# W_out's preparation, additions to the total, decodings, dense sums and last token pieces at other places of the phases

## The chip, the cores and the metric

The kernel runs on one core of one Trainium2 chip. The metric is the device time of one execution in microseconds (us), as the median of several runs of the same program. The engines are called PE (matrix multiplication), DVE (the vector engine), ACT (the scalar engine), POOL (GpSimd) and SP (the engine whose queue issues the kernel's DMAs). Each engine works through its own list of instructions in order.

## The reference, cut to what matters

Three layers follow each other: a linear attention with a decaying state, a mixture of 8 experts in which every expert sees every token, and a dense layer with a leaky activation.

```python
def reference(...):
    x = _attn_ref(q, k, v)              # (2, 8, 768, 64) -> 1536 tokens x 512
    x = _moe_ref(x, w_gate, w1, w2)
    return _moe2_ref(x, w_in, w_out, alpha)

def _moe_ref(x, w_gate, w1, w2):        # N 1536, D 512, E 8, F 1024
    P = np.exp(logits - logits.max())   # then 8 rounds of row and column scaling
    for e in range(E):
        h = np.maximum(x @ w1[e], 0.0)
        out += P[:, e:e + 1] * (h @ w2[e])

def _moe2_ref(x, w_in, w_out, alpha):   # d_ff 2048
    h = x @ w_in
    g = np.maximum(h, 0.0) + alpha * np.minimum(h, 0.0)
    return (g @ w_out).astype(np.float32)
```

## The kernel before

After the attention, the work is cut into 20 phases. Phases 0 to 7 are the experts for the 768 tokens of batch 0 and phases 8 to 15 the experts for those of batch 1. Phases 16 and 17 are the two halves of the dense layer for batch 0, phases 18 and 19 those for batch 1. `E` is 8, so `ph == E + 3` is phase 11. Phases from 8 on are called fast: there both matrix products are done with seven block products where eight would be needed, and every number is split in a high and a low part, so that one product is three matmuls (high by high, high by low, low by high).

A fast phase has 56 positions, and each holds six matmuls of 128x128 by 128x384 columns. Positions 0 to 26 and 29 are the products of the first layer, called (j, p) with j from 0 to 3 and p from 1 to 7; positions 27, 28 and 30 to 55 are those of the second layer, numbered u from 0 to 27 (`fast2`). Product (j, 6) makes a partial result E out of bank B by a DVE addition (line 931), and (j, 7) goes on adding into bank B, so PE has to wait until DVE has read it. In the same way DVE evacuates (j, 7) from B (line 940) before (j, 4) adds to it.

All other work hangs on positions. `step(ph, pos, fn)` says that `fn` is recorded behind the matmuls of that position. This sets only the order in which each engine's instructions stand in its queue; when one runs follows from its queue and from what it waits for. A fast phase's other work is:

- `decode_at`: one unit of W_in or W_out, which comes as 64-bit numbers, is turned into float32. Its four positions are for three DVE passes (lines 832, 834, 837), one ACT pass (842), two DVE passes (850, 853), and a store that also starts the load of the next unit (858, 822). The buffer `rd` that the next unit lands in is a single one. There are 32 units, 18 of them in phases 8 to 15.
- `dense_prep(i)`, i from 0 to 7 for phases 8 to 15: a quarter of a half of W_out is loaded (248), split on ACT and DVE (253, 257) and stored (275, 276), then four sums are made on POOL (267), split again, and stored (273). Its six positions are for the load, the high part with a store, the low part with a store, the four sums, the second high part and the second low part.
- `gather(m, h)`: an expert's weighted result `t` is added to `total` on POOL (1075), eight such additions a phase, in the phase after the one that made them.
- `t1` to `t4` (990, 995 or 997, 1009) make the second layer's combined inputs from the hidden blocks b11, b12, b21 and b22 on DVE; `hhigh(k)` (1017, ACT) and `hlow(k)` (1025, DVE) split input k, of 14, into the tile `hs`, which has five buffers. Input k is used by u = 2k and u = 2k + 1. In the dense phases the activation costs another ACT pass (902) and DVE pass (903) for each block.
- `x_keep(3, ...)`: the tokens of batch 1 for the dense layer, the last token pieces. Fourteen pieces are made in phases 16 and 17 from `total`: a POOL subtraction (349), a high part on ACT (353), a low part on POOL (357), a store (360). The tile `xs` of these pieces has two buffers. `x_fetch` (365) loads the finished pieces at the end of phase 17. `x_keep(2, ...)` does the same for batch 0 in phases 9 to 14.
- `w1_at`: the next phase's first-layer weights. In phases 15 to 19 they need four POOL sums each (`w1_sum`, 129).

```python
        def step(ph, pos, *fns):
            if pos >= 60:
                ph, pos = ph + 1, pos - 60
            for fn in fns:
                at(ph, seq[ph][pos], fn)
```

Of the kernel before, what the change touches and what calls it, by code (L numbers as in the profile page):

```python
# [23 lines left out]
E, F = 8, 1024  # L24
# [22 lines left out]
def tile_kernel(ctx, tc, lead, qkT, kv, ctab, w_gate, w1, w2, w_in, w_out, alpha, out):  # L47
# [349 lines left out]
    with tc.manual_schedule():  # L397
# [774 lines left out]
# [5 lines that stand above are left out]
# [27 lines left out]
        for ph in range(len(PHASES)):  # L1204
# [28 lines left out]
            if fast:  # L1233
                w1_at(ph, n + 2, pool, dve, 0, 3, 4, 4, 6, 9, 10)
                w1_at(ph, n + 3, pool, dve, 5, 10, 12, 11, 13, 16, 17)
                w1_at(ph, n + 4, pool, dve, 24, 36, 38, 39, 40, 42, 43)
                w1_at(ph, n + 5, pool, dve, 34, 44, 45, 48, 49, 50, 52)
            else:
# [27 lines left out]
            if fast:  # L1266
                if ph in (E + 3, E + 6):
                    decode_at(ph, 4, 5, 6, 8)
                    decode_at(ph, 13, 14, 15, 17)
                    decode_at(ph, 24, 25, 26, 28)  # L1270
                else:
                    decode_at(ph, 5, 7, 8, 10)
                    decode_at(ph, 19, 21, 23, 25)
                if E + 1 < ph < 2 * E:
                    for q in range(8):
                        step(ph, (2, 5, 8, 11, 14, 17, 20, 24)[q], lambda m=q // 2, h=q % 2: gather(m, h))
                if ph < 2 * E:
                    step(ph, 0, lambda ph=ph: weight_load(ph))
                    if ph == E:
                        keys = ((ph, 6), (ph, 13), (ph, 24), (ph, 27), (ph, 36), (ph, 40))  # L1280
                    elif ph == E + 1:
                        keys = ((ph - 1, 50), (ph, 3), (ph, 14), (ph, 15), (ph, 24), (ph, 27))
                    else:
                        keys = ((ph - 1, 38), (ph - 1, 46), (ph, 2), (ph, 3), (ph, 20), (ph, 23))
                    for (q, pos), fn in zip(keys, dense_prep(ph - E)):
                        step(q, pos, fn)
                dense = ph >= 2 * E
                p2, p3, q3 = (24, 33, 35) if dense else (21, 25, 31)
                for pos, fn, jp in ((17, t1, 0), (p2, t2, 0), (p3, t3, 0), (27, t1, 1), (30, t2, 1), (q3, t3, 1)):
                    step(ph, pos, lambda ph=ph, fn=fn, jp=jp: fn(ph, jp))  # L1290
                h2, h4 = (21, 29) if dense else (19, 22)
                l2, l4 = (23, 30) if dense else (20, 24)
                highs = (11, 25, h2, 28, h4, 31, 32, 34, 36, 38, 41, 43, 47, 49)
                lows = (13, 26, l2, 29, l4, 32, 33, 35, 37, 39, 42, 44, 48, 50)
                for k in range(14):
# [6 lines left out]
                if ph == 2 * E:  # L1302
                    for k in range(2):
                        step(ph, 3 + k, lambda k=k: x3.append(x_keep(3, k, *x_copy(k, total))))
                    for i, key in enumerate((29, 33, 38, 42, 46, 50, 66, 73, 80, 86, 90, 94, 97, 100)):
                        for q, pos in enumerate((0, 2, 3, 5)):
                            to = key + pos
                            step(ph + to // 56, to % 56, lambda i=i, q=q: x3[i % 2][i // 2][q]())
# [8 lines left out]
            if ph + 1 in XGROUP:  # L1317
                g = XGROUP[ph + 1]
                if g > 1:
                    for i, pos in enumerate((20, 21, 22, 23, 25, 26, 28, 30, 38, 40, 45, 46, 50, 51)):  # L1320
                        q = (B11, T1, T2, B21, T3, T4, B22)[i // 2]
# [143 lines left out]
```

## Time and profile before

| | before |
|---|---|
| time, median of 3 runs | 1299.54 us (1299.24 to 1300.45) |
| the profiled execution, its time | 1297.32 us |
| the profiled execution, its span | 1295.6 us |
| PE busy | 1263.1 us (97%) |
| DVE busy | 1035.4 us (80%) |
| ACT busy | 632.6 us (49%) |
| POOL busy | 450.8 us (35%) |
| moved by DMA | 379.21 MB |

The span runs from the first to the last instruction of the profiled execution; its own time is 1.7 us longer, and it lies 2.2 us under the median of the runs. A busy share is an average over stages with different limits. Because PE does the same matmuls in each fast phase, a phase that is longer than the shortest one shows by how much PE was made to wait or ran slower.

### The profile page before, as it was taken

The page shows a single profiled execution, that of the slowest core. Times are in us where ns is not written, and L with a number is a line of the kernel's source. Part 1 is how long each engine was busy: PE and PEld are TensorE (multiplying, and loading weights), DVE is VectorE, ACT ScalarE, POOL GpSimd, SP SyncE. Part 2 cuts the span into 40 slices and gives each one's busy share as a digit, 9 for nine tenths or more (in the row PEclk, how much of TensorE's full clock was granted, in tenths as well). Part 3 has the DMA queues.
Part 4 walks back from the last instruction along what each step waited for, and adds up shares of the span by engine and source line. Part 5 has one row for each costly group of instructions (what it writes and reads, how often), then busy time and mean ns, then how long its engine had stood idle before and what let it go on. Part 6 is the DMA issues. An engine that isn't in the chain of part 4 may idle for free.

```text
span 1295.6 us, 20588 instructions
## 1 busy us (share of the span) xinstructions
PE 1263.1 (97%) x7358; PEld 1192.6 (92%) x7358; DVE 1035.4 (80%) x1546; ACT 632.6 (49%) x1153; POOL 450.8 (35%) x414
## 2 busy tenths in 40 slices
PE   9999999999999999999999999999899998989998
PEld 7889898989898989899999999999899998979998
DVE  6677888988888888657779787879787978686867
ACT  5634543435352625354546453546354455645653
POOL 5734161707071625001123413242404435554110
PEclk9999999999999999999999999999999999998999
DMA  9785999999999999799897989899798956687625
GB/s 357 263 262 158 329 340 336 340 332 348 337 342 341 337 332 338 251 367 345 280 393 250 377 279 337 279 322 305 272 329 280 341 196 211 230 278 256 181 81 179
DMA packets 231158, 379.21 MB, mean 293 GB/s; under 512 B 16992, under 2 KB 135824, under 8 KB 231056
## 3 DMA queue, kind: packets, MB, share of 16 engines
q1 hardware_dynamic: 231056, 377.90, 85.7%
q8 instruction: 58, 0.95, 0.3%
q14 instruction: 44, 0.36, 0.1%
HBM read 243.59 MB, written 132.67 MB: 290 GB/s over the span
## 4 chain that ended last, share of the span: by engine, by line
PE 73%; DVE 12%; DMA 7%; issue 4%; ACT 2%; SPq 1%; POOL 1%; DVEq 0%; ACTq 0%; POOLq 0%
PE B L288 8%; PE B L289 8%; PE B L290 8%; PE o L288 5%; PE o L290 5%; PE o L289 5%; PE A L289 5%; PE A L288 5%; PE A L290 5%; PE D L290 3%; PE E L288 3%; PE E L289 3%; PE E L290 3%; PE D L288 3%; PE D L289 3%
## 5 line engine op out<-in xcount | busy, mean ns | idle before, releaser
L1017 ACT ACTIVATE hs<-b 128x768 fp32r<-128x768 f32 x168 | 140.2, 842 | 92.4 <-DVE b L990 43.3
L1025 DVE TENSOR_TENSOR hs<-b,hs 128x768 fp32r<-128x768 f32 x144 | 154.4, 1077 | 19.8 <-ACT hs L1017 18.7
L129 POOL TENSOR_TENSOR raw<-raw 128x256 f32<-128x256 f32 x136 | 133.6, 992 | 104.9 <-DMA raw<-wd 46.9
L288 PE MATMUL B<-xh,W 128*128 128x384 f32 x440 | 150.0, 341 | 7.5 <-DVE E L931 4.0
L290 PE MATMUL B<-xh,W 128*128 128x384 f32 x440 | 147.8, 336 | 0.0
L289 PE MATMUL B<-xl,W 128*128 128x384 f32 x440 | 147.7, 336 | 0.0
L224 POOL TENSOR_TENSOR pr<-pr 128x256 f32<-128x256 f32 x52 | 51.9, 999 | 190.4 <-DMA pr<-in_w_dram 62.9
L149 ACT ACTIVATE W<-raw 128x512 fp32r<-128x512 f32 (+1 forms) x144 | 98.5, 694 | 19.4 <-DVE raw L129 19.3
L288 PE MATMUL A<-xh,W 128*128 128x384 f32 x320 | 107.6, 336 | 0.0
L290 PE MATMUL A<-xh,W 128*128 128x384 f32 x320 | 107.4, 335 | 0.0
L289 PE MATMUL A<-xl,W 128*128 128x384 f32 x320 | 107.1, 335 | 0.0
L288 PE MATMUL B<-hs,ws 128*128 128x384 f32 x288 | 97.9, 340 | 8.9 <-ACT hs L1017 7.3
L289 PE MATMUL B<-hs,ws 128*128 128x384 f32 x288 | 97.8, 340 | 1.8 <-DVE hs L1025 1.8
L928 ACT ACTIVATE B<-A 128x384 f32<-128x384 f32 x80 | 38.3, 478 | 123.9 <-PE A L290 120.4
L1075 POOL TENSOR_TENSOR total<-total,t 128x384 f32<-128x384 f32 x54 | 73.8, 1390 | 67.3 <-DVE t L1055 64.2
L290 PE MATMUL B<-hs,ws 128*128 128x384 f32 x288 | 97.1, 337 | 0.0
L931 DVE TENSOR_TENSOR E<-B,d 128x384 f32<-128x384 f32 x80 | 45.1, 563 | 64.8 <-PE B L290 58.7
L267 POOL TENSOR_TENSOR dr<-dr 128x256 f32<-128x256 f32 x32 | 29.3, 917 | 190.7 <-DVE dw L257 147.7
L288 PEld LDWEIGHTS B<-xh,W 128*128 128x128 f32 x440 | 82.7, 188 | 12.8 <-DVE E L931 6.8
L159 POOL TENSOR_TENSOR W<-raw,W 128x512 fp32r<-128x512 f32 (+1 forms) x49 | 76.3, 1572 | 38.2 <-ACT W L149 19.2
L159 DVE TENSOR_TENSOR W<-raw,W 128x512 fp32r<-128x512 f32 (+1 forms) x95 | 86.8, 929 | 2.8 <-ACT W L149 2.8
L289 PEld LDWEIGHTS B<-xl,W 128*128 128x128 f32 x440 | 82.8, 188 | 0.3
(492 smaller groups left out, 3690.4 us busy)
## 6 DMA issues: line engine op xcount, KB each, us to landing
ws<-c SPq DMA_DIRECT2D x168, 512.0 KB, 6.5
raw<-in_w_dram SPq DMA_DIRECT2D x64, 512.0 KB, 5.8
c<-W SPq DMA_DIRECT2D x64, 384.0 KB, 6.5
W<-c SPq DMA_DIRECT2D x88, 256.0 KB, 6.4
pr<-in_w_dram SPq DMA_DIRECT2D x32, 512.0 KB, 6.1
c<-pw SPq DMA_DIRECT2D x32, 512.0 KB, 7.2
c<-pr SPq DMA_DIRECT2D x32, 512.0 KB, 7.9
raws<-in_w_dram SPq DMA_DIRECT2D x32, 384.0 KB, 5.7
```

Source lines behind the costliest of these rows:

```text
L129: eng.tensor_tensor(out=out, in0=in0, in1=in1, op=op)
L149: nc.scalar.activation(out=hi, in_=src, func=AF.Copy)
L159: eng.tensor_tensor(out=lo, in0=src, in1=hi.bitcast(F32), op=ALU.subtract)
L224: eng.tensor_tensor(out=out, in0=in0, in1=in1, op=op)
L288: nc.tensor.matmul(ps, ah, bh, start=first, stop=False, skip_group_check=True)
L289: nc.tensor.matmul(ps, ah, bl, start=False, stop=False, skip_group_check=True)
L290: nc.tensor.matmul(ps, alo, bh, start=False, stop=last, skip_group_check=True)
L928: nc.scalar.activation(out=banks[n, "B"], in_=banks[n, "A"], func=AF.Copy)
L931: nc.vector.tensor_tensor(out=banks[n, "E"], in0=banks[n, "B"], in1=banks[n, "d"], op=add)
L1017: nc.scalar.activation(out=t[:, 0, :], in_=hsource(ph, k), func=func)
L1025: nc.vector.tensor_tensor(out=lo, in0=src, in1=hi.bitcast(F32), op=ALU.subtract)
L1075: eng.tensor_tensor(out=dst, in0=dst, in1=tt[m, h], op=ALU.add)
```

## The change

All edits are numbers of positions, and rules by phase that choose them. No operation is added or taken away.

- The POOL sums of the next phase's first-layer weights stand at 18 and 28 and no longer at 24 and 34.
- Three units are decoded in phases 8 and 9, no longer in 11 and 14. In 8 and 9 they begin at positions 5, 17 and 29.
- The eight additions to the total stand in pairs at 2, 5, 8 and 11, no longer one by one up to 24.
- W_out's preparation has the same six positions in all its phases, 6, 12, 24, 27, 40 and 52. From phase 10 on its load and first split stood in the phase before, and its sums at 3.
- In the dense phases `t2` and `t3` and the parts of inputs 2 and 4 stand where they stand in the expert phases.
- The last token pieces begin at 8 of phase 16, no longer at 29, with wider spaces, and end at 42 of phase 17 and no longer at 49. The last pieces of a group of tokens are fetched at up to 46 and no longer up to 51.

```diff
             if fast:
...
-                w1_at(ph, n + 4, pool, dve, 24, 36, 38, 39, 40, 42, 43)
-                w1_at(ph, n + 5, pool, dve, 34, 44, 45, 48, 49, 50, 52)
+                w1_at(ph, n + 4, pool, dve, 18, 36, 38, 39, 40, 42, 43)
+                w1_at(ph, n + 5, pool, dve, 28, 44, 45, 48, 49, 50, 52)
...
-                if ph in (E + 3, E + 6):
-                    decode_at(ph, 4, 5, 6, 8)
-                    decode_at(ph, 13, 14, 15, 17)
-                    decode_at(ph, 24, 25, 26, 28)
+                if ph < E + 2:
+                    decode_at(ph, 5, 7, 8, 10)
+                    decode_at(ph, 17, 18, 19, 21)
+                    decode_at(ph, 29, 30, 31, 33)
                 else:
                     decode_at(ph, 5, 7, 8, 10)
                     decode_at(ph, 19, 21, 23, 25)
                 if E + 1 < ph < 2 * E:
                     for q in range(8):
-                        step(ph, (2, 5, 8, 11, 14, 17, 20, 24)[q], lambda m=q // 2, h=q % 2: gather(m, h))
+                        step(ph, (2, 5, 8, 11)[q // 2], lambda m=q // 2, h=q % 2: gather(m, h))
                 if ph < 2 * E:
                     step(ph, 0, lambda ph=ph: weight_load(ph))
-                    if ph == E:
-                        keys = ((ph, 6), (ph, 13), (ph, 24), (ph, 27), (ph, 36), (ph, 40))
-                    elif ph == E + 1:
-                        keys = ((ph - 1, 50), (ph, 3), (ph, 14), (ph, 15), (ph, 24), (ph, 27))
-                    else:
-                        keys = ((ph - 1, 38), (ph - 1, 46), (ph, 2), (ph, 3), (ph, 20), (ph, 23))
-                    for (q, pos), fn in zip(keys, dense_prep(ph - E)):
-                        step(q, pos, fn)
-                dense = ph >= 2 * E
-                p2, p3, q3 = (24, 33, 35) if dense else (21, 25, 31)
-                for pos, fn, jp in ((17, t1, 0), (p2, t2, 0), (p3, t3, 0), (27, t1, 1), (30, t2, 1), (q3, t3, 1)):
+                    for pos, fn in zip((6, 12, 24, 27, 40, 52), dense_prep(ph - E)):
+                        step(ph, pos, fn)
+                for pos, fn, jp in ((17, t1, 0), (21, t2, 0), (25, t3, 0), (27, t1, 1), (30, t2, 1), (31, t3, 1)):
                     step(ph, pos, lambda ph=ph, fn=fn, jp=jp: fn(ph, jp))
-                h2, h4 = (21, 29) if dense else (19, 22)
-                l2, l4 = (23, 30) if dense else (20, 24)
-                highs = (11, 25, h2, 28, h4, 31, 32, 34, 36, 38, 41, 43, 47, 49)
-                lows = (13, 26, l2, 29, l4, 32, 33, 35, 37, 39, 42, 44, 48, 50)
+                highs = (11, 25, 19, 28, 22, 31, 32, 34, 36, 38, 41, 43, 47, 49)
+                lows = (13, 26, 20, 29, 24, 32, 33, 35, 37, 39, 42, 44, 48, 50)
...
-                    for i, key in enumerate((29, 33, 38, 42, 46, 50, 66, 73, 80, 86, 90, 94, 97, 100)):
+                    for i, key in enumerate((8, 12, 20, 25, 31, 37, 43, 49, 66, 70, 78, 85, 89, 93)):
                         for q, pos in enumerate((0, 2, 3, 5)):
                             to = key + pos
                             step(ph + to // 56, to % 56, lambda i=i, q=q: x3[i % 2][i // 2][q]())
...
-                    for i, pos in enumerate((20, 21, 22, 23, 25, 26, 28, 30, 38, 40, 45, 46, 50, 51)):
+                    for i, pos in enumerate((20, 21, 22, 23, 25, 26, 28, 30, 34, 36, 42, 43, 45, 46)):
```

Three places show how the queues change. The first is DVE's queue in phase 8, from position 16 to 22, before: `rd1_7_1` is the second unit that is decoded in the phase, `b110_8` becomes the combined input, and `b221_8` is the evacuation of product (2, 7) from bank B.

```order
L159 TENSOR_TENSOR W_144<-raws_5485,W_144 128x256
L990 TENSOR_TENSOR b110_8_6076<-b120_8_6160,b110_8_6076 128x768
L940 TENSOR_TENSOR b221_8_6256<-B34_6195,d34_6207 128x384
L832 TENSOR_SCALAR ex1_7_1_6267<-rd1_7_1_6175 128x512
L834 TENSOR_SCALAR a1_7_1_6269<-rd1_7_1_6175 128x512
L837 SCALAR_TENSOR_TENSOR a1_7_1_6269<-rd1_7_1_6175,a1_7_1_6269 128x512
L1025 TENSOR_TENSOR hs8_2_6272<-b110_8_6076,hs8_2_6272 128x768
L995 SCALAR_TENSOR_TENSOR b110_8_6076<-b220_8_6092,b110_8_6076 128x768
L931 TENSOR_TENSOR E35_6304<-B35_6265,d35_6281 128x384
```

With the change the same stretch of DVE's queue reads:

```order
L159 TENSOR_TENSOR W_144<-raws_5485,W_144 128x256
L832 TENSOR_SCALAR ex1_7_1_6249<-rd1_7_1_6175 128x512
L834 TENSOR_SCALAR a1_7_1_6251<-rd1_7_1_6175 128x512
L837 SCALAR_TENSOR_TENSOR a1_7_1_6251<-rd1_7_1_6175,a1_7_1_6251 128x512
L990 TENSOR_TENSOR b110_8_6076<-b120_8_6160,b110_8_6076 128x768
L940 TENSOR_TENSOR b221_8_6261<-B34_6195,d34_6211 128x384
L850 SCALAR_TENSOR_TENSOR a1_7_1_6251<-a1_7_1_6251,al_74,ex1_7_1_6249 128x512
L853 SCALAR_TENSOR_TENSOR a1_7_1_6251<-rd1_7_1_6175,a1_7_1_6251 128x512
L1025 TENSOR_TENSOR hs8_2_6275<-b110_8_6076,hs8_2_6275 128x768
L995 SCALAR_TENSOR_TENSOR b110_8_6076<-b220_8_6092,b110_8_6076 128x768
L931 TENSOR_TENSOR E35_6309<-B35_6271,d35_6284 128x384
```

The three passes over `rd1_7_1` moved ahead of line 990 and ahead of the evacuation in line 940.

The second place is POOL's queue in phase 10 before. The `t9` tiles are phase 9's results, which are added to `total`, `dr2` is the piece of W_out, and `xs2` is a token piece of batch 0.

```order
L1075 TENSOR_TENSOR total_955<-total_955,t9_00_7105 128x384
L267 TENSOR_TENSOR dr2_7067<-dr2_7067 128x256 x4
L1075 TENSOR_TENSOR total_955<-total_955,t9_01_7193 128x384
L1075 TENSOR_TENSOR total_955<-total_955,t9_10_7117 128x384
L1075 TENSOR_TENSOR total_955<-total_955,t9_11_7206 128x384
L1075 TENSOR_TENSOR total_955<-total_955,t9_20_7230 128x384
L1075 TENSOR_TENSOR total_955<-total_955,t9_21_7147 128x384
L357 TENSOR_TENSOR xs2_0_1_7438<-b1_2_0_6655,xs2_0_1_7438 128x384
L1075 TENSOR_TENSOR total_955<-total_955,t9_30_7240 128x384
L1075 TENSOR_TENSOR total_955<-total_955,t9_31_7163 128x384
```

With the change POOL's queue in phase 10 reads:

```order
L1075 TENSOR_TENSOR total_955<-total_955,t9_00_7123 128x384
L1075 TENSOR_TENSOR total_955<-total_955,t9_01_7207 128x384
L1075 TENSOR_TENSOR total_955<-total_955,t9_10_7135 128x384
L1075 TENSOR_TENSOR total_955<-total_955,t9_11_7220 128x384
L1075 TENSOR_TENSOR total_955<-total_955,t9_20_7246 128x384
L1075 TENSOR_TENSOR total_955<-total_955,t9_21_7165 128x384
L1075 TENSOR_TENSOR total_955<-total_955,t9_30_7256 128x384
L1075 TENSOR_TENSOR total_955<-total_955,t9_31_7177 128x384
L357 TENSOR_TENSOR xs2_0_1_7455<-b1_2_0_6664,xs2_0_1_7455 128x384
L267 TENSOR_TENSOR dr2_7339<-dr2_7339 128x256 x4
```

The four sums of W_out's preparation moved from the head of this stretch to its end, and nothing stands between the eight additions.

The third place is SP's queue near the end of phase 17 before: `ws17` are weights of the second layer, `y17` results that go out, `xs3` last token pieces that are stored, `xh3_3` and `xl3_3` the two parts of the piece T4 that are fetched. Stores of `xs3_0_3` and `xs3_1_3` make up that piece.

```order
L1036 DMA ws17_12_12002<-c2_9_121 128x2x512
L1071 DMA out_0_dram<-y17_00_12013 128x384
L1036 DMA ws17_13_12024<-c2_9_121 128x2x512
L1071 DMA out_0_dram<-y17_10_12026 128x384
L360 DMA xc3_123<-xs3_1_3_11992 128x2x384
L114 DMA raw0_74_12033<-wd0_2_127 128x1024
L365 DMA xh3_3_12053<-xc3_123 128x768
L1071 DMA out_0_dram<-y17_21_12063 128x384
L360 DMA xc3_123<-xs3_0_2_12030 128x2x384
```

With the change SP's queue has the store of the same piece ten rows ahead of its fetch:

```order
L360 DMA xc3_123<-xs3_1_3_11896 128x2x384
L365 DMA xh6_3_11934<-xc3_123 128x768
L1036 DMA ws17_9_11943<-c2_9_121 128x2x512
L365 DMA xl6_3_11935<-xc3_123 128x768
L1036 DMA ws17_10_11968<-c2_9_121 128x2x512
L360 DMA xc3_123<-xs3_0_2_11947 128x2x384
L1036 DMA ws17_11_11989<-c2_9_121 128x2x512
L1036 DMA ws17_12_12011<-c2_9_121 128x2x512
L1071 DMA out_0_dram<-y17_00_12021 128x384
L360 DMA xc3_123<-xs3_1_2_11993 128x2x384
L365 DMA xh3_3_12027<-xc3_123 128x768
```

The fetch of T4 stood two rows behind the store that it needs, and stands ten rows behind it now.

## Rows read from the trace of the kernel before

**Rows 1.** Windows by phase: length, busy PE, PEld, DVE, ACT, POOL, clock, DMA.

```profile
549.00:612.24 63.24, 60.59 (x352) 59.58 (x351) 45.03 (x66) 31.24 (x57) 5.33 (x4) 1.00 0.98 346
612.24:671.03 58.79, 58.62 (x337) 58.33 (x337) 45.27 (x62) 30.57 (x54) 10.30 (x10) 1.00 0.93 331
671.03:730.64 59.61, 58.77 (x337) 58.31 (x337) 50.27 (x62) 29.62 (x53) 20.51 (x17) 1.00 0.89 315
730.64:792.98 62.34, 59.51 (x337) 58.23 (x337) 50.01 (x67) 29.84 (x52) 15.79 (x13) 1.00 0.90 311
792.98:853.49 60.51, 59.01 (x337) 58.25 (x337) 50.25 (x62) 29.62 (x53) 20.25 (x17) 1.00 0.91 315
...
913.10:977.65 64.55, 60.78 (x337) 59.78 (x337) 50.83 (x67) 29.72 (x52) 15.16 (x13) 0.97 0.87 300
977.65:1038.43 60.78, 59.07 (x338) 58.33 (x337) 53.85 (x64) 29.32 (x51) 32.36 (x25) 1.00 0.85 292
1038.43:1103.95 65.52, 60.83 (x338) 58.08 (x337) 53.38 (x65) 35.82 (x64) 28.21 (x26) 1.00 0.65 217
1103.95:1174.61 70.66, 62.79 (x338) 60.23 (x337) 54.63 (x69) 36.18 (x65) 37.79 (x33) 0.95 0.73 248
1174.61:1233.26 58.65, 58.62 (x337) 58.30 (x337) 44.62 (x63) 34.10 (x59) 14.59 (x16) 1.00 0.68 220
```

**Rows 2.** Waits of PE from 549 us on: total us, times, longest.

```profile
PE B L288 <- ACT hs L1017: 7.3, 3, 4.1
PE B L288 <- DVE E L931: 6.4, 8, 1.2
PE B L288 <- DVE b L940: 3.3, 2, 2.1
```

**Rows 3.** Timeline, DVE and PE, phase 8: start, duration, engine, line.

```profile
573.16 0.56 DVE L940 TENSOR_TENSOR b<-B,d 128x384 f32<-128x384 f32 x1
575.16 0.43 DVE L832 TENSOR_SCALAR ex<-rd 128x512 uint32<-128x512 uint32 x1 [1.45 <-DMA rd<-in_w_out_dram]
575.96 0.69 DVE L837 SCALAR_TENSOR_TENSOR a<-rd,a 128x512 f32<-128x512 uint32 x1
575.04 0.33 PE L288 MATMUL B<-xh,W 128*128 128x384 f32 x1
```

**Rows 4.** Windows, behind PE's wait of 2.1 us in phase 14.

```profile
941.20:944.20 3.00, 3.00 (x11) 3.00 (x10) 1.72 (x3) 1.20 (x2) 0.00 (x0) 0.50 0.85 202
```

**Rows 5.** Timeline, DVE and POOL, phase 10.

```profile
693.53 1.39 DVE L837 SCALAR_TENSOR_TENSOR a<-rd,a 128x512 f32<-128x512 uint32 x1
692.02 2.35 POOL L1075 TENSOR_TENSOR total<-total,t 128x384 f32<-128x384 f32 x2
```

**Rows 6.** Timeline, POOL, DVE and PE, phase 8, positions 27 to 31.

```profile
581.64 5.57 POOL L267 TENSOR_TENSOR dr<-dr 128x256 f32<-128x256 f32 x4 [71.96 <-DVE dw L257]
583.72 1.48 DVE L1025 TENSOR_TENSOR hs<-b,hs 128x768 fp32r<-128x768 f32 x1
585.25 0.44 PE L289 MATMUL A<-hs,ws 128*128 128x384 f32 x1 [0.43 <-DVE hs L1025]
```

**Rows 7.** Timeline, ACT and SP, phases 16 and 17.

```profile
1099.46 0.52 ACT L353 ACTIVATE xs<-b 128x384 fp32r<-128x384 f32 x1 [7.92 <-DMA xc<-xs]
1159.84 0.38 SPq L360 DMA_DIRECT2D xc<-xs  x1
1166.03 0.33 SPq L365 DMA_DIRECT2D xh<-xc  x1
1166.05 0.52 ACT L353 ACTIVATE xs<-bb 128x384 fp32r<-128x384 f32 x1 [9.17 <-DMA xc<-xs]
```

**Rows 8.** Timeline, DVE and PE, phase 18, positions 23 to 30.

```profile
1199.15 0.57 DVE L931 TENSOR_TENSOR E<-B,d 128x384 f32<-128x384 f32 x1 [1.45 <-PE B L290]
1204.54 0.96 DVE L1025 TENSOR_TENSOR hs<-b,hs 128x768 fp32r<-128x768 f32 x1
1206.39 0.34 PE L289 MATMUL A<-hs,ws 128*128 128x384 f32 x1
```

## The prediction, made before the changed kernel had run

> **What bounds the kernel now.** I began with the shares of busy time: PE is busy for 97% of the span, so the time can only change where PE waits or runs slower. Second came the windows by phase [rows 1]. Every fast phase holds the same matmuls, so its length is a gauge. Phase 18 takes 58.65 us, of which PE is busy 58.62: that is a phase without loss. The others exceed it by 0.14 (phase 9), 0.96 (10; phase 13 has the same length of 59.61, so one row stands for both), 3.69 (11), 1.86 (12), 5.90 (14), 2.13 (15), 6.87 (16) and 12.01 us (17). Together phases 9 to 17 lose 34.5 us. Phase 8 has transposes of its own and serves only as its own reference. Third, the waits of PE [rows 2] say who causes the loss: DVE, where it evacuates a bank late (lines 931 and 940), and ACT, where it makes `hs` late (line 1017). PE's wait is the last link in each case, so for every edit I asked what it does to DVE's and ACT's queues at those places.
>
> **The change part by part.** No instruction is added or removed; each cost below is a wait that appears or goes.
>
> *Third decoding in phase 8: +5.0.* Now DVE evacuates (2, 7) at 573.16 and only then waits 1.45 us for the unit's data, which come at 575.16 [rows 3]. With the change the three passes stand ahead, so DVE waits for the data with the evacuation behind it. Nothing ahead of that load moves in SP's queue, so I leave the arrival at 575.16. The three passes take until 576.65 (575.96 and 0.69), line 990 about 0.96 (the length of a 128x768 pass alone [rows 8]), the evacuation 0.56: 578.2. PE wants the bank at 575.04 [rows 3]. Its wait is then about 3.1 us; I take 3.0, since passes overlap slightly. Behind the 2.1 us wait of phase 14, PE's granted clock was 0.50 for 3.00 us [rows 4], the lower of its two levels, 1.2 GHz, so half of that time, 1.5, was lost. I add 1.5 here. For the unit at position 29 I add 0.5: five more passes (1.49 and two of at most 0.96) fall among the splits of the second layer, but the 3 us wait has given DVE time. Bounds: 1.5 if the data come 1.5 us earlier and the clock stays, 8 if the last unit costs all its 3.4.
>
> *Third decoding in phase 9: +1.1.* There is no such late arrival to see in this phase (its loss is 0.14). The unit at 29 is in front of the split of input 3, and the sums of W_out's preparation now run beside it. Bounds 0 and 3.
>
> *Phases 10 to 14: -9.4.* They lose 13.37 us (0.96, 3.69, 1.86, 0.96, 5.90). In phase 10 a decoding pass that takes 0.69 alone [rows 3] takes 1.39 while POOL adds to the total [rows 5]; behind it DVE reaches the partial result E late. PE waited for that eight times, 6.4 us, and 3.3 us for line 940 [rows 2]. With the change the eight additions stand together, and the sums no longer stand in front of seven of them. POOL can so make them at the end of the phase before and in the first positions, ahead of the decodings. The third unit goes from 11 and 14. What comes new is the four sums at position 27. Phase 8 has them there already: they take 5.57 us on POOL, a split beside them takes 1.48 instead of 0.96, and PE waits 0.43 for it [rows 6, 8]. I take 0.8 of loss for each of the five phases, 4.0 in all, twice the 0.43 because additions to the total move into the phase's tail. Bounds: 0.4 each (-11.4) and 1.7 each (-4.9).
>
> The Trainium skill, "SBUF — State Buffer", section "Who interferes with whom", says that a DVE instruction with two SBUF inputs and a GpSimd instruction that reads SBUF exclude each other, and that the later one waits for the whole of the earlier. The rows do not go so far: 1.48 for a pass of 0.96 beside POOL instructions of 1.39 (5.57 by four) is half a microsecond more, not 1.39. By that rule the four sums would cost up to 5.6 us a phase; what follows from such a price is the third rival.
>
> *Phase 15: +0.6.* The second split's low part at 52 puts a DVE pass of about 1.3 us (128x1024 against 0.96 for 128x768) into a half where DVE is busiest (53.85 us in the phase [rows 1]). Bounds -0.5 and 2.5.
>
> *Phase 16: -5.2.* The last token pieces have two buffers, so ACT's high part of piece i waits until the store of piece i - 2 has landed, and ACT's `hs` parts stand behind it. ACT stood 7.92 us that way [rows 7]. Pieces are 4 positions apart there, two are some 8 us, and a store alone takes 6.2 (1159.84 to 1166.03 [rows 7]), with POOL and SP's queue before it. With the change they are 5 to 8 apart, and six of eight begin before position 38. A remaining 1.7 us is DVE's: POOL's sums and pieces now run beside the splits of inputs 1 and 3. Bounds -6.9 (all) and -1.
>
> *Phase 17: -10.5.* Here the chain is the same, and a fetch adds to it: the store of T4 is issued at 1159.84, its fetch goes out only at 1166.03, and ACT restarts at 1166.05 after 9.17 us [rows 7]. That was PE's longest wait, 4.1 us [rows 2], and the clock fell (0.95 in the window [rows 1]). With the change the store stands ten rows ahead of its fetch and the last piece seven positions earlier. I leave 1.5 us. Bounds -12 and -5.
>
> *Dense sums: 0.* In phase 18 `t2` and two splits come earlier. DVE has 1.45 us idle ahead of E, and ends the split of input 1 at 1205.50, 0.9 before PE reads it at 1206.39 [rows 8]. The idle time takes one pass and half the other, so E is about 0.5 late, inside the 0.9. Without this cover it is 0.5 in each of four phases. Bounds -0.5 and 4.
>
> *Fetches and first-layer sums: 0.* The sums wait for their load, not for their place: POOL has only these sums in phases 18 and 19. The fetches gain about 5 us of room ahead of the next group.
>
> Sum: 5.0 + 1.1 - 9.4 + 0.6 - 5.2 - 10.5 = -18.4. The profiled execution took 1297.3 us, so it would take 1278.9. The median of the runs is 2.2 above it: 1281.1, rounded to 1281.
>
> **The rivals.** *Half the chain stays.* The pieces still have two buffers; if POOL's queue makes each late, ACT waits at positions 31 to 41 in place of 43 to 54. For it speaks that POOL now has four first-layer sums (about 5.6 us) at 28, right ahead of the pieces; against it that the spaces are wider than store and split together. Half of 15.7 comes back: 1289.
>
> *No effect.* Places order queues only; where an instruction waits for data, it runs as before. If DVE's load, not its order, makes the losses, phases 8 and 9 lose what 11 and 14 gain, and 16 and 17 keep theirs: about 1299. Against it speaks that ACT's long waits end with a store, not with DVE.
>
> *Slower: the sums at position 27.* In phases 9 to 15 the four sums fall on the splits that PE waits for next. Should each of four splits be delayed by a whole sum (1.39 us) and only 1.6 be absorbed, each of seven phases would lose 4.0, 28 in all, where the forecast allows 4.0 together: 1281 + 24 = 1305. From (18.4 + 4.0) / 7 = 3.2 us a phase on, the kernel is slower than before. For it speaks how rows 6 show a split stretched; against it that phase 8 has just this arrangement and loses 0.43.
>
> **How the numbers follow.** Chances: forecast 0.70, half the chain 0.13, no effect 0.05, sums at 27 0.12. About 2.6 us, 0.2%, can be told from no change. Faster takes forecast and half the chain, less 0.02 for mixtures: 0.81; the same 0.06; slower 0.13. The bounds of all terms would give -29.8 and +6.6 if all met; they don't, so downward I take two thirds of the distance from the forecast (11.4 by 2/3 is 7.6, about 1273), and upward I go to 1297, which holds half the chain and most mixtures and leaves out slower and part of no effect, with the low tail under 2 in 10. The forecast's own range is 1273 to 1288.
>
> **What would show it.** In the changed kernel's trace: one PE wait of about 3 us on line 940 in phase 8, with DVE waiting for `rd` ahead of it, and a stretch at half clock behind; phases 10 to 14 near 59.5 us each with no wait on line 931 over 0.5; no ACT wait of over 3 us on the stores of `xs`; phases 16 and 17 near 60.3 us. The prediction is wrong if PE waits for the splits at positions 30 to 36 by more than 2 us in several phases, or if ACT still stands behind the stores of the token pieces.

## The result, and the profile after

The changed kernel takes 1281.86 us (median of 4 runs, 1281.14 to 1283.34), the kernel before took 1299.99 us (4 runs, 1299.24 to 1300.66) beside it. The ratio is 0.9862, with a 95% interval from 0.9845 to 0.9879. The profiled execution took 1283.34 us, with a span of 1281.6 us.

The windows by phase of the changed kernel, phases 8 to 18, with the columns of [rows 1]:

```profile
549.71:618.17 68.46, 62.39 (x352) 61.15 (x350) 48.39 (x72) 32.34 (x58) 4.73 (x4) 0.98 0.93 325
618.17:678.52 60.35, 59.20 (x337) 58.23 (x337) 49.55 (x66) 30.32 (x54) 17.30 (x13) 1.00 0.93 320
678.52:736.91 58.39, 58.39 (x337) 58.39 (x337) 47.05 (x64) 29.42 (x53) 22.73 (x18) 1.00 0.94 329
736.91:795.28 58.37, 58.37 (x337) 58.37 (x337) 44.63 (x63) 28.98 (x51) 17.09 (x14) 1.00 0.93 312
795.28:853.89 58.61, 58.61 (x338) 58.31 (x337) 45.87 (x62) 29.47 (x53) 21.66 (x18) 1.00 0.93 325
853.89:912.87 58.98, 58.65 (x337) 58.33 (x337) 46.75 (x64) 29.35 (x53) 22.55 (x18) 1.00 0.93 318
912.87:971.27 58.40, 58.40 (x338) 58.40 (x337) 44.60 (x63) 28.86 (x51) 17.30 (x14) 1.00 0.92 315
971.27:1032.99 61.72, 59.30 (x337) 58.24 (x337) 49.74 (x63) 30.24 (x52) 28.11 (x23) 1.00 0.87 300
1032.99:1096.18 63.19, 60.97 (x338) 59.69 (x337) 54.05 (x67) 37.04 (x67) 33.69 (x32) 0.97 0.78 252
1096.18:1160.13 63.95, 60.33 (x338) 58.02 (x338) 54.24 (x69) 34.49 (x61) 27.90 (x27) 1.00 0.75 258
1160.13:1219.31 59.18, 59.16 (x338) 58.21 (x338) 46.09 (x63) 33.81 (x59) 15.89 (x18) 1.00 0.66 221
```

Against [rows 1], phase 8 grew by 5.22 us and phase 9 by 1.56; phases 10 to 14 went from 306.62 to 292.75 us together and have almost no loss left; phase 15 grew by 0.94, phase 16 shrank by 2.33 and phase 17 by 6.71; phase 18 grew by 0.53. That sums to -14.7 us. The spans differ by 14.0 us, the medians by 18.1: the profiled execution of the changed kernel is the longest of its four, and that of before, at 1297.32 us, lay 2.7 us under the median of 1299.99. The terms below are read from the profiles and so carry an uncertainty of a few us in their sum.

PE's waits in the changed kernel from 549 us on (total us, times, longest), which answer to [rows 2]:

```profile
PE B L288 <- DVE b L940: 4.4, 3, 3.1
PE A L289 <- DVE hs L1025: 4.2, 3, 1.9
PE B L289 <- DVE hs L1025: 3.0, 4, 1.0
PE B L288 <- DVE E L931: 2.3, 4, 1.1
```

The waits for ACT (line 1017, 7.3 us) are gone. What is new is one long wait on line 940, which is in phase 8. The waits for DVE's low parts of the splits (line 1025) are not new: in the kernel before they were 4.9 us together, more than those on line 940, and [rows 2] leaves them out:

```profile
PE A L289 <- DVE hs L1025: 3.1, 4, 1.1
PE B L289 <- DVE hs L1025: 1.8, 3, 0.7
```

They have grown to 7.2 us, and they are in phases 9 and 15 to 17.

The wait in phase 8, DVE's timeline in the changed kernel (compare [rows 3]), then PE's, and the window behind it (compare [rows 4]):

```profile
577.10 0.43 DVE L832 TENSOR_SCALAR ex<-rd 128x512 uint32<-128x512 uint32 x1 [3.13 <-DMA rd<-in_w_out_dram]
577.90 0.69 DVE L837 SCALAR_TENSOR_TENSOR a<-rd,a 128x512 f32<-128x512 uint32 x1
578.51 0.95 DVE L990 TENSOR_TENSOR b<-b,b 128x768 f32<-128x768 f32 x1
579.38 0.55 DVE L940 TENSOR_TENSOR b<-B,d 128x384 f32<-128x384 f32 x1
```

```profile
579.99 0.68 PE L288 MATMUL B<-xh,W 128*128 128x384 f32 x1 [3.14 <-DVE b L940]
```

```profile
580.00:583.00 3.00, 3.00 (x9) 3.00 (x10) 2.93 (x4) 1.21 (x3) 0.00 (x0) 0.50 1.04 392
```

DVE waits 3.13 us for the unit's data, the evacuation stands three passes and line 990 behind it, PE waits 3.14 us for the evacuation, and then PE runs at half clock for 3 us.

ACT's waits from 1030 to 1180 us, the one line of the kernel before and the three longest of the changed kernel:

```profile
ACT xs L353 <- DMA xc<-xs: 18.6, 3, 9.2
```

```profile
ACT B L928 <- PE A L290: 24.3, 3, 12.3
ACT n L902 <- DVE b L940: 10.9, 9, 2.6
ACT hs L1017 <- DVE b L990: 9.3, 2, 4.9
```

ACT no longer waits for a store of a token piece. It waits for PE and DVE instead.

### The profile page after: what moved, and what is told of

Same layout as the page of the kernel before. It is cut to its first block, busy times and chain, and to the rows that moved or that the text cites. A ratio compares the mean times of both kernels' runs of the same rounds, so it can differ in the third digit from the quotient of the medians.

```text
span 1281.6 us, 20569 instructions
## 1 busy us (share of the span) xinstructions
PE 1260.6 (98%) x7358; PEld 1193.4 (93%) x7358; DVE 1015.4 (79%) x1546; ACT 630.3 (49%) x1153; POOL 456.6 (36%) x414
## 4 chain that ended last, share of the span: by engine, by line
PE 78%; DVE 11%; DMA 5%; issue 3%; ACT 2%; SPq 1%; POOL 1%; DVEq 0%; ACTq 0%; POOLq 0%
PE B L288 9%; PE B L289 9%; PE B L290 9%; PE A L289 6%; PE A L290 5%; PE A L288 5%; PE o L288 5%; PE o L290 5%; PE o L289 5%; PE D L288 3%; PE D L289 3%; PE D L290 3%; PE E L288 3%; PE E L290 3%; PE E L289 3%
## 5 line engine op out<-in xcount | busy, mean ns | idle before, releaser
L129 POOL TENSOR_TENSOR raw<-raw 128x256 f32<-128x256 f32 x136 | 129.7, 964 | 121.9 <-DMA raw<-wd 71.3
L1025 DVE TENSOR_TENSOR hs<-b,hs 128x768 fp32r<-128x768 f32 x144 | 148.7, 1039 | 11.8 <-ACT hs L1017 11.4
L289 PE MATMUL B<-hs,ws 128*128 128x384 f32 x288 | 96.8, 336 | 3.0 <-DVE hs L1025 3.0
L357 POOL TENSOR_TENSOR xs<-b,xs 128x384 fp32r<-128x384 f32 x21 | 28.7, 1365 | 198.5 <-ACT xs L353 198.5
L288 PE MATMUL B<-hs,ws 128*128 128x384 f32 x288 | 96.4, 335 | 0.1
L290 PE MATMUL B<-hs,ws 128*128 128x384 f32 x288 | 96.3, 334 | 0.0
L1075 POOL TENSOR_TENSOR total<-total,t 128x384 f32<-128x384 f32 x54 | 70.9, 1341 | 69.9 <-DVE t L1055 66.9
L159 DVE TENSOR_TENSOR W<-raw,W 128x512 fp32r<-128x512 f32 (+1 forms) x95 | 82.8, 887 | 3.3 <-ACT W L149 3.3
L267 POOL TENSOR_TENSOR dr<-dr 128x256 f32<-128x256 f32 x32 | 42.4, 1326 | 115.3 <-DVE dw L257 100.3
```

The source lines that it names most:

```text
L129: eng.tensor_tensor(out=out, in0=in0, in1=in1, op=op)
L159: eng.tensor_tensor(out=lo, in0=src, in1=hi.bitcast(F32), op=ALU.subtract)
L267: nc.gpsimd.tensor_tensor(out=out, in0=in0, in1=in1, op=op)
L288: nc.tensor.matmul(ps, ah, bh, start=first, stop=False, skip_group_check=True)
L289: nc.tensor.matmul(ps, ah, bl, start=False, stop=False, skip_group_check=True)
L290: nc.tensor.matmul(ps, alo, bh, start=False, stop=last, skip_group_check=True)
```

## The experiments

The runs came in three groups, each beside the kernel before, whose medians were 1297.74, 1299.39 and 1299.51 us. So kernels of different groups are compared by their ratios to before; 0.001 is 1.3 us. The changed kernel has 0.9862.

### One part undone at a time

**Decodings as before** (u_dec), three in phases 11 and 14, none of the other edits undone:

```diff
-                if ph < E + 2:
-                    decode_at(ph, 5, 7, 8, 10)
-                    decode_at(ph, 17, 18, 19, 21)
-                    decode_at(ph, 29, 30, 31, 33)
+                if ph in (E + 3, E + 6):
+                    decode_at(ph, 4, 5, 6, 8)
+                    decode_at(ph, 13, 14, 15, 17)
+                    decode_at(ph, 24, 25, 26, 28)
```

> The changed kernel with the decodings where they were: two units in phases 8 and 9, three in 11 and 14. Theory (order: the third unit of phase 8 costs because DVE waits for its data with the evacuation of (2, 7) behind it): the wait of 3.1 us in phase 8 goes, and phases 8 and 9 come back to 63.2 and 59 us, 6.6 us less. In 11 and 14 the units are no longer stretched by additions to the total, so they lose about 1 us each there: 1281.9 - 6.6 + 2 = 1277. Rival (load: three units in a phase cost what they cost wherever they stand): 11 and 14 lose 3.7 and 5.9 again, 1281.9 - 6.6 + 9.6 = 1285.

Measured: 1292.76 us, 0.9956 [0.9939, 0.9973]. Neither theory held. Phases 8 and 9 gave back what was expected (phase 9 is 58.40 us long), but phases 11 and 14 took 67.90 and 67.42 us, longer than in the kernel before. DVE and PE of that kernel in phase 11, timelines:

```profile
748.01 0.43 DVE L832 TENSOR_SCALAR ex<-rd 128x512 uint32<-128x512 uint32 x1 [4.59 <-DMA rd<-in_w_in_dram]
...
750.29 0.56 DVE L931 TENSOR_TENSOR E<-B,d 128x384 f32<-128x384 f32 x1
```

```profile
750.90 0.45 PE L288 MATMUL B<-xh,pairs 128*128 128x384 f32 x1 [2.43 <-DVE E L931]
```

The second unit stands at 13, five positions behind the issue of its data at 8, and W_out's load, now at 6, goes out 1.5 us ahead of it on the same queue (740.33 and 741.87). DVE waits 4.59 us for the data with E behind it. A second wait, 3.12 us for a split, follows in the same phase, where POOL makes W_out's four sums. Both waits return in phase 14 (2.26 and 3.05 us). POOL, DVE and PE at the second one:

```profile
762.03 5.05 POOL L267 TENSOR_TENSOR dr<-dr 128x256 f32<-128x256 f32 x4 [9.71 <-DVE dw L257]
766.43 1.47 DVE L1025 TENSOR_TENSOR hs<-b,hs 128x768 fp32r<-128x768 f32 x1
767.96 0.69 PE L289 MATMUL A<-hs,ws 128*128 128x384 f32 x1 [3.12 <-DVE hs L1025]
```

This gave a new theory: the old decodings and the new load of W_out don't fit together. The next group tests it.

**Token pieces and fetches as before** (u_pieces):

```diff
-(8, 12, 20, 25, 31, 37, 43, 49, 66, 70, 78, 85, 89, 93)
+(29, 33, 38, 42, 46, 50, 66, 73, 80, 86, 90, 94, 97, 100)
...
-(20, 21, 22, 23, 25, 26, 28, 30, 34, 36, 42, 43, 45, 46)
+(20, 21, 22, 23, 25, 26, 28, 30, 38, 40, 45, 46, 50, 51)
```

> The changed kernel with the last token pieces and their fetches where they were, from position 29 of phase 16 to 49 of phase 17. Theory (two buffers, so the pieces' stores hold up ACT): ACT waits of 7 to 9 us on the stores of xs come back, phases 16 and 17 lengthen from 127 us to 136 or more: 1291 to 1294. Rival (it was the other edits that helped phases 16 and 17): 1282, phases 16 and 17 together within 2 us of 127.

Measured: 1288.91 us, 0.9931 [0.9912, 0.9949]: about 9 us lost. Phase 17 is back at 70.21 us, and ACT waits 19.4 us for the stores again. Phase 16 takes 63.88 us, only 0.69 more than in the changed kernel.

**W_out's preparation and the additions to the total as before** (u_prepgat): the six `keys` rules of the diff and the additions at `(2, 5, 8, 11, 14, 17, 20, 24)`.

> The changed kernel with W_out's preparation and the additions to the total where they were. Theory (POOL's work beside the decodings delays DVE, and so the partial result E): waits on line 931 come back in phases 10 to 14, about 1 to 1.5 us in each, 1281.9 + 6 = 1288. Rival (in phases 10 to 14 only the third unit of 11 and 14 mattered): 1282, phases 10 to 14 stay near 58.5 us.

Measured: 1287.19 us, 0.9917 [0.9904, 0.9929], about 7 us lost, the time that the theory gives. In phases 10, 12 and 13 PE waits for E again, 0.83 to 0.84 us each time, and they take 59.61, 60.93 and 59.61 us. In phases 11 and 14 no such wait returns: without the third unit they stay at 58.74 and 59.04 us.

**Dense sums and the splits of inputs 2 and 4 as before** (u_t): the lines with `dense`, `h2` and `l2` of the diff, put back.

> The changed kernel with the dense phases' combined inputs and the parts of inputs 2 and 4 where they were (24, 33, 35, and 21 to 30). Theory (in phases 16 and 17 DVE is late for the split of input 1 because two more passes now stand in front of it, stretched by POOL): the waits of 1.9 and 1.5 us at u = 2 go, with the stretch at the lower clock behind the first, 1281.9 - 5 = 1277. Rival (the prediction's: the earlier places cost nothing, since DVE was idle there): 1282. Rival 2 (later places meet the token pieces and make phases 16 and 17 worse): 1284 or more.

Measured: 1280.01 us, 0.9854 [0.9839, 0.987]. The interval holds the changed kernel's 0.9862, so the whole time doesn't tell, but the phases do: 16 and 17 take 61.83 and 62.51 us in place of 63.19 and 63.95, and phase 18 is back at 58.67. The edit is no gain. DVE's timeline in phase 16 of the changed kernel, what PE then met, and the window behind it:

```profile
1057.55 0.96 DVE L1025 TENSOR_TENSOR hs<-b,hs 128x768 fp32r<-128x768 f32 x1 [0.36 <-ACT hs L1017]
1058.54 0.96 DVE L997 TENSOR_TENSOR b<-b,b 128x768 f32<-128x768 f32 x1
1059.42 0.56 DVE L931 TENSOR_TENSOR E<-B,d 128x384 f32<-128x384 f32 x1
...
1066.11 1.47 DVE L1025 TENSOR_TENSOR hs<-b,hs 128x768 fp32r<-128x768 f32 x1
```

```profile
1067.64 0.44 PE L289 MATMUL A<-hs,ws 128*128 128x384 f32 x1 [1.89 <-DVE hs L1025]
```

```profile
1067.70:1071.20 3.50, 3.50 (x12) 3.50 (x13) 2.56 (x3) 1.20 (x2) 3.14 (x3) 0.56 0.31 112
```

The same two places with the dense sums as before (phase 16 begins 0.62 us later there), and PE behind them:

```profile
1058.88 0.57 DVE L931 TENSOR_TENSOR E<-B,d 128x384 f32<-128x384 f32 x1 [1.04 <-PE B L290]
...
1065.08 1.30 DVE L1025 TENSOR_TENSOR hs<-b,hs 128x768 fp32r<-128x768 f32 x1
```

```profile
1066.43 0.45 PE L289 MATMUL A<-hs,ws 128*128 128x384 f32 x1 [0.16 <-DVE hs L1025]
```

In the changed kernel a split and a sum stand ahead of E's evacuation, which comes 1.16 us later in the phase. The later split, which runs beside four POOL sums, then ends late: PE waits 1.89 us and works on at half clock, against a wait of 0.16 us.

The half clock does not follow from the wait alone. Five other runs that keep the dense edit (u_dec, u_prepgat, u_decprep, u_gat and d_1114) have the same wait at this place, 1.89 or 1.90 us, and their clock stayed at 1.00; in a_unit19 it fell, as here. The window behind it in u_dec:

```profile
1078.90:1082.40 3.50, 3.50 (x21) 3.50 (x21) 2.55 (x3) 1.21 (x2) 3.14 (x3) 1.00 0.33 107
```

Their phase 16 takes 61.78 to 62.41 us, at most 0.6 more than with the dense sums as before. The differences in phases 17 and 18 stand in every profile: 63.95 to 64.01 and 59.18 to 59.24 us in those five and the changed kernel. So the edit costs 2 to 2.5 us where the clock stays and 3.3 where it falls.

### Where the third decoding stands

**The new positions, but in phases 11 and 14** (d_1114), one line: `if ph in (E + 3, E + 6):` ahead of 5, 17, 29.

> The changed kernel with its own three decoding positions (5, 17, 29), but in phases 11 and 14, where the kernel before had its third decoding, in place of phases 8 and 9. Theory (the place within the phase decides: the unit at 13 stood too close behind the fetch of its data, which the early fetch of W_out's block holds up; 12 positions between two units give the fetch time): phases 11 and 14 stay under 60.5 us, phases 8 and 9 lose their waits of 3.1 and 0.7 us (7.3 us together against the changed kernel, as in the run with the old decodings): about 1277, ratio to the kernel before 0.982. Rival (a phase in which W_out is prepared has no room on VectorE for a third decoding, wherever it stands): phases 11 and 14 near 67 as with the old decodings, about 1291, ratio 0.994.

Measured: 1280.8 us, 0.9854 [0.9834, 0.9874]. Phases 11 and 14 take 60.80 and 60.34 us, not 67, so the rival falls: it is the place within the phase. The profiled run, with 1278.75 us the fastest of five, comes within 2 us of the theory's 1277; the median lies further off, and against the changed kernel the gain is inside the intervals. One wait of 1.62 us on line 940 is left in each of the two phases.

**Decodings and W_out's preparation as before** (u_decprep), both diffs above without the additions.

> The changed kernel with the decodings and W_out's preparation as before (the additions to the total stay at 2, 5, 8, 11). Theory (old decodings and the new early fetch of W_out's block collide): phases 11 and 14 come back from 67.9 and 67.4 to 60 to 63 us, phases 8 and 9 as in the kernel before without its chain: about 1283, ratio 0.987. Rival (the third decoding in phases 11 and 14 costs 9 us a phase by itself once the additions stand early): stays near 1292, ratio 0.995.

Measured: 1283.28 us, 0.9872 [0.9852, 0.9892], the time that the theory gives, 11 us better than with the decodings alone undone. Phases 11 and 14 take 62.86 and 62.39 us, phases 10, 12 and 13 58.36 to 58.39. Undoing a second part mends most of what undoing the first one broke. But the load of W_out is not what makes the difference. The second unit's data and the split in phase 11, DVE and PE:

```profile
749.31 0.43 DVE L832 TENSOR_SCALAR ex<-rd 128x512 uint32<-128x512 uint32 x1 [2.73 <-DMA rd<-in_w_in_dram]
...
765.55 0.95 DVE L1025 TENSOR_TENSOR hs<-b,hs 128x768 fp32r<-128x768 f32 x1
```

```profile
766.55 0.44 PE L289 MATMUL A<-hs,ws 128*128 128x384 f32 x1 [0.74 <-DVE hs L1025]
```

No load of W_out goes out ahead of the unit's here, and yet DVE gets the data 18.61 us into the phase, against 18.48 in u_dec, and makes E 20.88 us into it, against 20.76. The 5.0 us between the two kernels in this phase arise behind that, at the split and behind it. In u_dec the split pass of line 257 (1.22 us) stands behind the third unit's first passes, and the passes of lines 850 and 853 and the split take 1.22, 1.10 and 1.47 us beside POOL's four sums; here they take 0.68, 0.69 and 0.95, the sums stand at 3, and line 257 runs ahead of the unit, in time in which DVE waits for its data. Behind the wait of 3.12 us the clock was 0.50 for 4.0 us besides. This is read from the two traces; no run moves the sums alone.

**The second unit of phase 8 two positions later** (a_unit19): 19, 20, 22, 23 in phase 8.

> The changed kernel with the second decoding of phase 8 at 19, 20, 22, 23 in place of 17, 18, 19, 21. Theory (the wait of 3.1 us in phase 8 is the evacuation queued behind the decoding's wait for its data, which land at 575.2 us): the wait and the half clock behind it go, phase 8 from 68.5 to about 64 us, 1277.4, ratio 0.983. Rival (the wait moves on to the next evacuation behind position 19, or to the third decoding at 29 whose data are then fetched 2 positions later): phase 8 stays within 1 us of 68.5, 1281 to 1283, ratio 0.986.

Measured: 1279.63 us, 0.9843 [0.9823, 0.9863]. The wait of 3.14 us is gone and phase 8 takes 63.96 us (549.65 to 613.61), as the theory says. The whole gained only half of these 4.5 us, and the interval just reaches the changed kernel's ratio: phases 10 to 14 took 1.2 us more in that profile.

**The first layer's sums on POOL as before** (u_w1): 24 and 34 in place of 18 and 28.

> The changed kernel with the first layer's sums on GpSimd at 24 and 34, as before, in place of 18 and 28. Theory (these sums cost nothing at either place): 1281 to 1283, ratio 0.986. Rival 1 (at 18 and 28 they stand ahead of the dense sums on GpSimd and make input 3's split late, waits of 1.9 and 1.5 us in phases 16 and 17): 1278, ratio 0.983. Rival 2 (at 24 and 34 the sums are late for their VectorE steps at 36 and 44): 1285, ratio 0.989.

Measured: 1283.53 us, 0.9872 [0.9851, 0.9894]. Between the theory and rival 2, and not to be told from no change. Rival 1 has its mechanism, but not its gain: the waits for the split in phases 16 and 17 become shorter (1.27 and 0.74 us), but waits for ACT of 0.90 and 1.39 us stand there instead, and the two phases take 62.98 and 64.45 us.

### Parts alone, and the sum

**The kernel before with the new token pieces and fetches only** (b_pieces), the second diff above the other way round.

> The kernel before with the changed kernel's positions of the last token pieces and of their fetches only. Theory (ScalarE's waits for the stores of the pieces are what phases 16 and 17 lose): 1290 to 1292, ratio 0.993, phase 17 from 70.7 to about 64 us, and ScalarE's waits of 18.6 us on the stores in phases 16 and 17 gone. Rival (the pieces help only beside the other moves): 1296 or more, ratio 0.998 to 1.0.

Measured: 1289.13 us, 0.9925 [0.9907, 0.9944], a little better than the theory. Phases 16 and 17 take 62.83 and 64.03 us, 2.69 and 6.63 less than before, and ACT has no wait for a store there. The part gives alone what it gives among the others.

**Only the additions to the total as before** (u_gat).

> The changed kernel with the additions to the total alone as before (2, 5, 8, 11, 14, 17, 20, 24). Theory (the additions on GpSimd beside the decodings make the evacuations late): waits of about 0.8 us for E return in four or more of phases 10 to 14, 1286 to 1287, ratio 0.990. Rival (the loss of 5 to 7 us of the run with both undone was W_out's preparation, the additions cost nothing): 1282, ratio 0.986.

Measured: 1291.23 us, 0.9942 [0.9923, 0.996], about 10 us lost, rather more than with W_out's preparation undone as well, though the two intervals overlap. The decoding's pass in line 837 from 670 to 975 us, by form (shortest, median, longest in ns), in the kernel before, in the changed one, and with the additions as before:

```profile
L837 DVE SCALAR_TENSOR_TENSOR a<-rd,a x12: 692/1110/1390, 679.4 to 945.5; 128x512 f32<-128x512 uint32 x12
```

```profile
L837 DVE SCALAR_TENSOR_TENSOR a<-rd,a x10: 691/693/694, 685.8 to 934.8; 128x512 f32<-128x512 uint32 x10
```

```profile
L837 DVE SCALAR_TENSOR_TENSOR a<-rd,a x10: 693/1041/1392, 683.2 to 940.7; 128x512 f32<-128x512 uint32 x10
```

With the additions in pairs not one pass is stretched. With the additions as before, five of the ten take 1.39 us, each beside an addition, and five take 0.69, so that the median of 1.04 is the time of no pass. That shows the cause of the stretch in [rows 5]. What it costs PE is another question, since in u_prepgat all ten passes are stretched (1.11 to 1.39 us) and less is lost. The longest of the waits that came back here, in phase 10, has another link. ACT's and PE's timelines of that kernel:

```profile
694.31 1.06 ACT L253 ACTIVATE dw<-dr 128x1024 fp32r<-128x1024 f32 x1 [4.12 <-DMA dr<-wd]
695.28 0.47 ACT L925 ACTIVATE d<-D 128x384 f32<-128x384 f32 x1
```

```profile
696.40 0.45 PE L288 MATMUL B<-xh,W 128*128 128x384 f32 x1 [1.52 <-DVE E L931]
```

W_out's split at 12 waits for a load issued at 6, and ACT's part of E is queued behind it. The changed kernel has this wait too, 2.28 us, and there it ends just in time. So the loss of 10 us holds at least the additions and this link, and the runs don't part them further.

**Both improvements of phase 8 with the dense sums as before** (best_b): a_unit19 and u_t together.

> The changed kernel with phase 8's second decoding at 19, 20, 22, 23 and the dense sums and the splits of inputs 2 and 4 as before. Theory (4.6 us from phase 8 at the start of phase 9, and 2.7 us in phases 16 and 17): 1275 to 1277, ratio 0.982. Rival (as much comes back as in the run with phase 8's unit alone, 1279.6): 1278 to 1280, ratio 0.984.

Measured: 1276.08 us, 0.9824 [0.9804, 0.9843], on the theory.

**The third decoding in phases 11 and 14, the middle unit there at 19, the dense sums as before** (best_a):

```diff
-                if ph < E + 2:
+                if ph in (E + 3, E + 6):
                     decode_at(ph, 5, 7, 8, 10)
-                    decode_at(ph, 17, 18, 19, 21)
+                    decode_at(ph, 19, 20, 22, 23)
                     decode_at(ph, 29, 30, 31, 33)
```

> The changed kernel with the third decoding in phases 11 and 14 in place of 8 and 9, their middle unit at 19, 20, 22, 23 in place of 17, 18, 19, 21, and the dense sums and the splits of inputs 2 and 4 as before. Theory (the places of the last runs add up: third decoding in phases 11 and 14 gave a profiled run 4.6 us under that of the changed kernel with waits of 1.62 us left in each, and two positions later those go; the dense sums as before gave 2.7 us in phases 16 and 17): 1275 to 1277, ratio 0.981 to 0.982. Rival (what one wait gives up the next takes: small waits of 0.4 to 0.9 us appear elsewhere, as in the run with phase 8's unit moved): 1280, ratio 0.985.

Measured: 1273.36 us (1271.55 to 1274.28), 0.9803 [0.9782, 0.9823], better than the theory and than both kernels: the interval ends below that of the changed kernel. Its windows of phases 9, 11, 14, 16 and 17:

```profile
614.82:673.21 58.39, 58.39 (x338) 58.39 (x337) 46.36 (x62) 29.70 (x53) 18.09 (x13) 1.00 0.94 325
...
731.57:789.96 58.39, 58.39 (x337) 58.38 (x337) 47.21 (x67) 29.24 (x52) 16.92 (x14) 1.00 0.95 327
...
907.04:965.62 58.58, 58.58 (x337) 58.34 (x337) 47.07 (x68) 29.07 (x52) 17.35 (x14) 1.00 0.96 327
...
1027.33:1089.09 61.76, 60.56 (x338) 57.95 (x337) 53.25 (x67) 37.11 (x67) 33.72 (x31) 1.00 0.79 249
1089.09:1151.57 62.48, 59.89 (x338) 58.04 (x337) 52.58 (x69) 34.72 (x61) 27.24 (x27) 1.00 0.79 273
```

Phases 11 and 14 hold a third unit (67 and 68 DVE instructions against 62 in phase 9) without any loss. What is left is in phases 15 to 17, which together lie about 10 us over three times 58.65.

## Why the prediction was right, and where its terms were off

The time (1281 forecast, 1281.86 measured) and the direction were right, and the mechanism of each large term was. The sizes were less good, and that the median was met to 1 us is in part luck. Single terms were off by up to 4.5 us, with both signs. Summed from the two profiles the phases give -14.7 us and not -18.4, a miss of 3.7. The medians differ by 18.1 because the profiled execution of before was faster than its median and that of the changed kernel slower.

- **Third decoding in phase 8, +5.0: 5.22.** The wait (3.0 forecast, 3.14 seen), its cause and the half clock behind it were as described, and moving the unit two positions took the wait away (63.96 us for the phase, 63.24 before). The assumption that the data arrive unmoved was wrong: DVE got them 27.39 us into the phase, not 26.16 [rows 1, 3], and PE wanted the bank about as much later. The 1.5 us for the clock are not certain: in u_gat, which has the same order in phase 8, PE waits 3.21 us there, the clock stays at 1.00, and the phase takes 66.42 us, 3.2 more than before; in u_t, u_pieces, u_prepgat and u_w1 it fell again. The window behind that wait:

```profile
578.70:581.70 3.00, 3.00 (x17) 3.00 (x18) 2.93 (x4) 1.19 (x3) 0.00 (x0) 1.00 1.04 392
```

- **Third decoding in phase 9, +1.1: 1.56**, two waits of 0.73 (line 940) and 0.43 us (the split of position 29).
- **Phases 10 to 14, -9.4: -13.9.** Both causes are shown. With W_out's preparation as before, phases 10, 12 and 13 take 59.61 to 60.93 us with the old additions (u_prepgat) and 58.36 to 58.39 with the paired ones (u_decprep); phases 11 and 14 take 62.86 and 62.39 us with the third unit and 58.74 and 59.04 without. So about 9 us are the third unit's and about 5 the rest. The size was off: I left 0.8 us a phase for W_out's sums at 27 and for additions in the phase's tail, and hardly anything was left. The sums at 27 run beside splits that are not late. The same rows answer the third rival, "slower: the sums at position 27": four of the five phases lost nothing at all, far from 3.2 us. The mechanism does exist where DVE is late, as the wait of 3.12 us in u_dec shows.
- **Phase 15, +0.6: 0.94.**
- **Phases 16 and 17, -5.2 and -10.5: -2.3 and -6.7.** The chain of stores was the cause: undone, 9 us come back by the ratios (7.0 in these two phases of the profile), and alone in the kernel before it gives 9.3 in the two phases. ACT's waits for stores fell from 18.6 us to none, so "half the chain stays" falls too. What failed is the 1.7 and 1.5 us that I left for DVE's waits: the phases lie 4.5 and 5.3 us over 58.65. They are waits for the splits above all (line 1025; 1.89 us in phase 16, 1.47 and 0.97 in 17), which [rows 2] leaves out and for which the prediction left too little. Of the miss, 1.4 us in phase 17 and 0 to 1.4 in phase 16, by the clock, is the dense sums. What makes the rest is not shown.
- **Dense sums, 0: +2 to +3.3.** The cover of 0.9 us was read in phase 18, the quietest of the three dense phases in [rows 1] (DVE busy 44.62 us, POOL 14.59), and used for phases 16 and 17, where DVE is busy for over 53 us and POOL runs token pieces and sums beside the splits. Even in phase 18 the edit cost 0.5.
- **Fetches and first-layer sums, 0:** no difference that the runs could tell for the sums (u_w1); the fetches were moved back only together with the token pieces.

The Trainium skill, "SBUF — State Buffer", section "Who interferes with whom", calls the ports that DVE and POOL share an exclusive lock, so that a pass would be held until the POOL instruction ahead of it has ended. The traces agree, more closely than the prediction allowed when it set 0.5 us against the 1.39 of a whole sum: a pass is held for what is left of the POOL instruction, not for its full length. In [rows 5] POOL's addition ends at 694.37 and the pass of line 837 at 694.92, 0.55 later. At the first unit of the same phase POOL's sums end at 680.01 and the pass at 680.56, again 0.55 later:

```profile
676.22 3.79 POOL L267 TENSOR_TENSOR dr<-dr 128x256 f32<-128x256 f32 x4 [10.52 <-DVE dw L257]
679.45 1.11 DVE L837 SCALAR_TENSOR_TENSOR a<-rd,a 128x512 f32<-128x512 uint32 x1
```

The prediction missed one thing altogether: the parts depend on each other. Undoing the decodings alone costs 12 us, although phases 8 and 9 get shorter by it. I had costed W_out's sums at 27 by what they do to the splits, and not by the passes of a third unit, which at the old positions meet the split pass at 24 and the sums at 27.

Open stays what holds phases 15 to 17 at 61.7 to 62.5 us in the best version, and how the loss of u_gat divides between the additions and ACT's wait for W_out's data.

## What to carry to other kernels

Where an in-order engine evacuates banks, look at what an operation placed ahead of an evacuation waits for: moving one decoding unit two positions took a wait of 3.14 us away. A cover read in a quiet stage is no cover in a busy one: read it in the stage where it is used. Parts of one schedule are not additive; undo pairs as well as single parts before a part is called good or bad.

## What the runs showed of the hardware

- A DVE pass of 128x512 (line 837) takes 0.69 us alone and up to 1.39 beside POOL additions; ordering POOL's work into other positions brought all ten passes back to 0.69. From phase 8 of the kernel before on, all nine stretched passes end 0.55 us after the POOL instruction that ran when they began, be it a sum or an addition. For the 32 splits of 128x768 that began beside a POOL instruction it is 0.81 to 0.82 us.
- Two waits of PE in the changed kernel, of 3.14 and 1.89 us, were each followed by a granted clock at or near its lower level (0.50 over 3.0 us, 0.56 over 3.5 us), which cost 1.5 us more in each place. At the same two places of other runs, waits of 3.21 us (u_gat) and of 1.89 to 1.90 us (five runs) were followed by a clock of 1.00. One profile doesn't give the price of such a wait.
- Phases 10 and 11, whose order the dense edit doesn't touch, took 58.4 us each in one profile and 59.1 in another: a difference of under a microsecond in one phase of one profile says nothing by itself. One that returns in every profile does, as the 0.5 us of phase 18.
